# A gated mix of local and full attention on one core: the front's projections sum both row halves in one PSUM bank, in four banks that then go to the scores

## Chip, core and metric

One core of a Trainium2 chip. The metric is the device time in microseconds (us), as the median of several runs; smaller is better. Engines: TensorE (PE; PEld is its weight load), VectorE (DVE), ScalarE (ACT), GpSimd (POOL) and SyncE (SP, which issues DMAs). Matmuls write into PSUM, which has eight banks of 512 fp32 values in each of 128 partitions; GpSimd doesn't read PSUM in this kernel.

## What is computed

For one sequence of 2048 tokens of width 512, two attention branches and a gate:

```python
g = sigmoid((x * gate_w).sum(-1))
# branch A: 32 heads of 16; each token attends to 8 tokens, 2 apart, at and before it
qkv = x @ A_wqkv;  a = softmax(scale * q . k[pos - 2*w], w = 0..7) . v;  a = a @ A_wo
# branch B: 32 query heads of 16, one key and value head, all 2048 keys, no mask
q = x @ B_wq;  k = x @ B_wk;  v = x @ B_wv
b = softmax(q . k * 16 ** -0.5) . v;  b = b @ B_wo
out = g * a + (1 - g) * b
```

The softmax subtracts the row maximum, so all 32 x 2048 x 2048 scores of branch B are formed twice: once for their row maxima, once for the exponentials.

## The kernel before

**The work.** A projection in fp32 accuracy is three matmuls of split parts (high x high, high x low, low x high; `three`, line 168) for each of four 128-row blocks of the contraction: twelve products. Queries of branch B are split again and stored to DRAM (`qd`), and come back "stacked" as units: a unit is four heads by 512 queries, 32 units in all, of which eight are held at a time (`qst`). For a unit, `max_mm` forms scores for maxima with 512 keys in the free dimension, DVE reduces them, and the maxima are transposed and written into two spare contraction rows of the unit (`shift_a` to `shift_d`), so that the score matmul of `exp_pair` already subtracts them. 2048 such maxima tiles (128 rows by 512 keys) are needed, 64 for each unit, before that unit's turn.

**The front** (about 29 to 279 us). A list `lumps` holds 14 projections of queries (lumps `("q", m)`) and 64 of branch A (`("a", gg, j)`; 384 columns, and for gg 0 eighteen more, B's values and the gate). Each of a lump's twelve products is cut into its lower and upper 64 contraction rows, which the two row halves of PE work on at the same time. `stream` (line 660) is a planner: it keeps a model clock for PE, ACT and DVE (`clk`) with the durations of line 45 (`T_R`, `T_EXP`, ...), and issues for each slot one product to each half. Lower halves of lump x go to the first bank of a two-bank tile, upper halves to its second (line 1004; tiles `pe0` and `pe1` in turn, `pm` for the last lump). Into this it puts work on maxima where the model clock says that a bank is free:
- a *pair* (`fill_pair`): two matmuls into `pm`, one 1024-wide DVE reduction;
- a *single* (`fill_one`): one matmul in place of one half's product, into `ps` or `po`, one 512-wide reduction;
- from lump ("a", 0, 4) on, a *difference* (`fill_diff`, `fill_sum`): with keys prepared as half sums and half differences of two key blocks (`half_keys`), max(a, b) is half sum + |half difference|; two matmuls into `pm`, two ACT `Abs` into `dd`, then two matmuls into `ps` and `po` in place of one half's product each, and two DVE instructions that add and reduce. A difference stands for four maxima tiles.

At a lump's end ACT and POOL evict it. A query (`queries_post`, line 196): one ACT copy of both banks, a POOL addition of the halves, an ACT copy to the high part, a POOL subtraction for the low part, two DMAs. Branch A (`a_post`, line 226): an ACT copy of each bank, POOL additions, and for every second token block a DMA to DRAM (`ad`). Work for POOL and DMAs is queued in `tasks` with a due time. POOL otherwise computes branch A's local attention from `ad` (`work`, `run_pool`), from when the first quarter of branch A is stored until long after the front.

**The loop** (279 to 1510 us), 512 steps s: for each of 16 key blocks of each unit, two score pairs with their exponentials (`exp_pair`, tiles `pe0` and `pe1`, 1024-wide ACT), and the weighted sums of the step before (`weighted`, 128-row fp32 matmuls into `po`). In a step the planner places the members in the order of line 1068: scores 0, a pair ("m2"), scores 1, a single ("m1"), then the weighted sums. `fill_ready` (line 803) lets a pair or single in when its bank is free by the model, or will be within `M2S` or `M1S`; `singles` (line 799) allows singles only while more maxima are left than two for each remaining step. Three blocks of four rows of output projections (`out_phase`, also through `stream`) stand between steps, a fourth is spread over the last steps.

The first values of a unit's maxima tile (`unit_tile`, line 301) are set by an ACT instruction for units 0 to 8.

Of the kernel before, what the change touches and what calls it, by code (L numbers as in the profile page):

```python
# [6 lines left out]
F32 = mybir.dt.float32  # L7
# [34 lines left out]
LEAD, M2S, M1S = 1.5, 0.5, 0.3  # L42


T_R, T_LAT, T_EXP, T_RED2, T_RED1, T_W, T_TTR = 0.23, 0.20, 0.92, 1.14, 0.61, 1.21, 0.66
# [3 lines left out]
def gated_mix_kernel(ctx, tc, xt, wa, wk, wq, wo_a, wo_b, out):  # L49
# [19 lines left out]
    eb = [pp.tile([P, 2, 512], F32, name=f"pe{k}") for k in range(2)]  # L69
    m2 = pp.tile([P, 2, 512], F32, name="pm")  # L70
    m1 = pp.tile([P, 512], F32, name="ps")
    po = pp.tile([P, 512], F32, name="po")

# [97 lines left out]
    def keys(t):  # L171
        pk = eb[t % 2][:, 0, :]
# [23 lines left out]
    def queries_post(m, bank):  # L196

        nonlocal pool
        settle("rest", 0)
        two = p0.tile([P, 2, 512], F32, name="two", tag="wqr", bufs=1)  # L200
        nc.scalar.activation(two, bank, AF.Copy)
        at = after("act", clk["pe"] + T_LAT, 0.92)
        own = p0.tile([P, 512], F32, name="qraw", bufs=1)
        nc.gpsimd.tensor_add(own, two[:, 0], two[:, 1])
        pool = max(pool, 1e3 * at) + 1400
        hi, lo = parts_of()

        def rest():
            nonlocal pool
            nc.scalar.activation(hi, own, AF.Copy)  # L210
            nc.gpsimd.tensor_sub(lo, own, hi.bitcast(F32))
            pool = max(pool, 1e3 * after("act", 0, 0.6)) + 1400
            queries_out(m, hi, lo)
            if m > 4 and m % 2 and len(stacked) < NB:
                stack(len(stacked))

        tasks.append((pool / 1e3, rest, (), "rest"))
# [8 lines left out]
    def a_post(gg, j, x):  # L226

        nonlocal pool
        (bank, key), n = front[x], GN + (0 if gg else VN)
        settle("add", 1)  # L230
# [4 lines left out]
        if gg == 0 and j < 3:  # L235
            two = wp.tile([P, GN + VN], F32, name="two", tag="aext", bufs=2)
        else:
            two = (p2 if j % 3 else pm)[0].tile([P, GN + VN], F32, name="two", tag=("two", "raw", "own")[j % 3], bufs=1)
        own = st[:, :, j % 2, :]
        nc.scalar.activation(own, bank[:, 0, :GN].rearrange("p (g n) -> p g n", g=GC), AF.Copy)  # L240
        nc.scalar.activation(two[:, :n], bank[:, 1, :n], AF.Copy)  # L241
        if gg == 0:
            nc.scalar.activation(vst[:, j, 0:DH], bank[:, 0, GN:GN + DH], AF.Copy)
            nc.scalar.activation(gate[:, 1, j:j + 1], bank[:, 0, GN + DH:GN + DH + 1], AF.Copy)
        at = after("act", clk["pe"] + T_LAT, 0.8 if gg else 1.2)
        free[key] = at + 0.1

        def rest():
            nonlocal pool
            nc.gpsimd.tensor_add(own, own, two[:, :GN].rearrange("p (g n) -> p g n", g=GC))  # L250
            if gg == 0:
                nc.gpsimd.tensor_add(vst[:, j, 0:DH], vst[:, j, 0:DH], two[:, GN:GN + DH])
                nc.gpsimd.tensor_add(gate[:, 1, j:j + 1], gate[:, 1, j:j + 1], two[:, GN + DH:GN + DH + 1])
            pool = max(pool, 1e3 * at) + (1000 if gg else 1450)
            if j % 2 == 1:
                dst = ad[gg * GC:(gg + 1) * GC, HALO:, :].rearrange("g (p j) n -> p g (j n)", j=NJ)
                tasks.append((pool / 1e3 + 0.5, lambda: nc.sync.dma_start(dst[:, :, (j - 1) * AN:(j + 1) * AN], st.rearrange("p g j n -> p g (j n)")), (), "store"))
            if j == NJ - 1:
                tasks.append((pool / 1e3 + 1.0, whole, (gg,)))

        tasks.append((at, rest, (), "add"))
# [35 lines left out]

    def fillable():
        return bool(half) or bool(slots) and slots[0][0] < len(stacked) and stacked[slots[0][0]] <= clk["pe"]

    def unit_tile(v):
        if v not in mx:
            mx[v] = wp.tile([P, 2, 2, 4, 4], F32, name="mx", bufs=3)
            if v <= NB:
                nc.scalar.activation(mx[v].rearrange("p b i t k -> p (b i t k)"), ident[:, 0:64], AF.Identity, scale=0.0, bias=mk[:, 6:7])
            left[v] = NF // NU
# [9 lines left out]
    def filled(v, n):  # L316
        left[v] -= n
        if not left[v]:
# [4 lines left out]
            nc.vector.transpose(mt, ms.rearrange("p b x y -> p (b x y)"))  # L323
            tasks.append((after("dve", 0, 0.66) + (2.0 if kcd and not pe else 0.1), shift_a, (v, mt)))

    def fill_pair(dst, key):
# [4 lines left out]
        nc.vector.tensor_reduce(m[:, :, pr, t, kc], dst, AX.X, ALU.max)  # L331
        free[key] = after("dve", after("pe", 0, T_R) + T_LAT, T_RED2) + 0.08
        filled(v, 2)

    def fill_one(dst=m1, key="m1"):
# [6 lines left out]
        nc.vector.tensor_reduce(m[:, odd, pr, t, kc:kc + 1], dst, AX.X, ALU.max)  # L342
        free[key] = after("dve", after("pe", 0, T_R) + T_LAT, T_RED1) + 0.08
        filled(v, 1)
# [18 lines left out]
    def half_keys(g):  # L363

        keys = ("m2", "m2") if g == 0 else ("m1", "po")
# [26 lines left out]
    def fill_diff():  # L392
# [5 lines left out]
        for odd in range(2):  # L398
            nc.scalar.activation(dd[0][:, odd], m2[:, odd, :], AF.Abs)  # L399
            ready_d[odd] = after("act", at, 0.52) + 0.1  # L400
        free["m2"] = ready_d[1]
        pend.extend([(v, pr, t, kc, 0), (v, pr, t, kc, 1)])

    def fill_sum():
# [4 lines left out]
        nc.vector.tensor_tensor_reduce(dd[0][:, odd], dst, dd[0][:, odd], 1.0, -FMAX, ALU.add, ALU.max, m[:, odd, pr, t, kc:kc + 1])  # L409
# [754 lines left out]
```

## Time and profile before

| | |
|---|---|
| median of 3 runs | 1527.74 us (1527.43 to 1530.11) |
| span of the profiled execution, first to last instruction | 1523.8 us |
| PE, ACT, DVE, POOL busy over the span | 98%, 82%, 81%, 68% |
| front (first planned slot to the first steps' scores) | 29 to 279 us |
| granted TensorE clock, mean | 0.997 |

The profile is one execution; its span lies 3.9 us under the median, and only the span is recorded of it. A row of the timeline gives start, length, engine, line, operation, output and inputs, how many such instructions were merged (x2), and in brackets how long the engine had been idle before it and what ended that. A row of the groups gives count, then busy time in us and mean ns of one, then the idle time before them with its releasers. A row of waits gives total us, how often, the longest. PE's ends are modelled, so spacing of starts says more than length.

### The profile page before, as it was taken

What the parts mean: (1) busy time and instruction counts of PE and PEld (TensorE: products, weight loads), DVE (VectorE), ACT (ScalarE), POOL (GpSimd) and SP (SyncE); (2) the same over time, 40 slices, a digit from 0 to 9 for tenths busy, and PEclk for the clock granted to TensorE, in tenths of its full rate; (3) what the DMA queues carried; (4) which work ended last, traced back from release to release, by engine and by line L of the source; (5) the groups of instructions that cost most, each with busy time, mean ns of one, the idle gap of its engine ahead of it and who ended that gap; (6) DMA issues with size and microseconds to landing.
All of it is one profiled execution on the core that took longest, in us unless ns stands there. A gap on an engine that the chain in (4) does not pass through costs nothing.

```text
span 1523.8 us, 28901 instructions
## 1 busy us (share of the span) xinstructions
PE 1489.5 (98%) x10920; PEld 706.1 (46%) x10920; DVE 1235.3 (81%) x1755; ACT 1243.8 (82%) x1590; POOL 1030.6 (68%) x1769
## 2 busy tenths in 40 slices
PE   7999999999999999999999999999999999999988
PEld 4989888533333333333333453333345335433333
DVE  5976666788888888889888998898899889888701
ACT  4558987889999899999999759999975995799774
POOL 7866988787888888888888888889887004100020
PEclk9999999999999999999999999999999999999999
DMA  6744223121121121120220112202201000000000
GB/s 216 202 119 131 90 75 126 33 75 47 50 76 47 41 75 44 43 76 22 66 77 14 65 33 68 68 12 69 69 19 33 1 1 16 15 2 2 1 1 28
DMA packets 43908, 85.63 MB, mean 56 GB/s; under 512 B 9520, under 2 KB 25960, under 8 KB 39672
## 3 DMA queue, kind: packets, MB, share of 16 engines
q1 hardware_dynamic: 36200, 44.00, 9.8%
q0 software_dynamic: 6560, 37.95, 7.5%
q8 instruction: 86, 1.41, 0.4%
q10 hardware_dynamic: 1008, 1.84, 0.3%
q14 instruction: 54, 0.44, 0.1%
HBM read 57.97 MB, written 25.25 MB: 55 GB/s over the span
## 4 chain that ended last, share of the span: by engine, by line
PE 89%; ACT 4%; DVE 4%; POOL 1%; issue 1%; DMA 1%; DVEq 0%; ACTq 0%; POOLq 0%
PE po L458 32%; PE pe L448 22%; PE pm L311 9%; PE ps L311 8%; PE pe L1004 8%; PE pe L709 4%; DVE mx L331 2%; ACT dd L399 2%; ACT pexp L450 1%; PE pm L766 1%; PE pm L390 1%; PE pe L174 1%; DVE mx L342 1%; PE po L390 0%; PE ps L390 0%
## 5 line engine op out<-in xcount | busy, mean ns | idle before, releaser
L450 ACT ACTIVATE pexp<-pe 128x1024 f32<-128x1024 f32 x1024 | 992.9, 1022 | 116.3 <-PE pe L448 116.0
L331 DVE TENSOR_REDUCE mx<-pm 128x2 f32<-128x1024 f32 x554 | 676.6, 1221 | 125.7 <-PE pm L311 120.4
L458 PE MATMUL po<-pexp,vst 128*32 128x512 f32 x4096 | 547.1, 606 | 0.6 <-DVE tt L472 0.5
L448 PE MATMUL pe<-qst,kst 64*128 64x512 f32 x2048 | 460.9, 448 | 6.8 <-ACT pexp L450 2.6
L448 PEld LDWEIGHTS pe<-qst,kst 64*128 64x128 f32 x2048 | 190.6, 184 | 506.7 <-ACT pexp L450 488.4
L342 DVE TENSOR_REDUCE mx<-ps 128x1 f32<-128x512 f32 x565 | 384.4, 680 | 5.7 <-PE ps L311 5.0
L311 PE MATMUL pm<-kst,qst 62*128 62x512 f32 x1122 | 235.7, 407 | 3.1 <-DVE mx L331 2.4
L311 PE MATMUL ps<-kst,qst 62*128 62x512 f32 x565 | 228.6, 405 | 0.7 <-DVE mx L342 0.7
L518 POOL TENSOR_TENSOR pr<-aext 128x256 f32<-128x256 f32 x256 | 182.0, 736 | 0.2
L578 POOL TENSOR_TENSOR oa<-oa,av 128x256 f32<-128x256 f32 x224 | 163.9, 732 | 15.4
L458 PEld LDWEIGHTS po<-pexp,vst 128*32 128x32 f32 x4096 | 80.7, 108 | 182.5 <-issue 170.7
L575 POOL TENSOR_TENSOR av<-aext,lg 128x256 f32<-128x256 f32 x224 | 139.3, 622 | 12.8
L484 POOL TENSOR_TENSOR rl<-rl,gate_t 128x16 f32<-128x16 f32 x31 | 6.8, 220 | 182.6 <-DVE rl L478 182.4
L311 PEld LDWEIGHTS pm<-kst,qst 62*128 62x128 f32 x1122 | 108.9, 186 | 24.7 <-DVE mx L331 21.3
L311 PEld LDWEIGHTS ps<-kst,qst 62*128 62x128 f32 x565 | 105.3, 186 | 22.4 <-DVE mx L342 18.4
L399 ACT ACTIVATE dd<-pm 128x512 f32<-128x512 f32 x166 | 92.2, 610 | 21.8 <-DVE mx L409 10.8
L1004 PE MATMUL pe<-wah,xh 64*128 64x384 f32 (+1 forms) x504 | 108.5, 338 | 0.0
L1004 PE MATMUL pe<-wal,xh 64*128 64x384 f32 (+1 forms) x504 | 108.5, 337 | 0.0
L1004 PE MATMUL pe<-wah,xl 64*128 64x384 f32 (+1 forms) x504 | 108.4, 337 | 0.0
L409 DVE CUSTOM_DVE_ANT_0 dd<-ps,dd 128x512 f32<-128x512 f32 x83 | 57.4, 692 | 58.8 <-PE ps L390 29.4
L524 POOL TENSOR_TENSOR tr<-pr 128x512 f32<-128x512 f32 x64 | 81.7, 1276 | 4.2
L250 POOL TENSOR_TENSOR stage<-stage,two 128x384 f32<-128x384 f32 x64 | 65.0, 1015 | 26.3 <-ACT two L241 13.4
(185 smaller groups left out, 1596.7 us busy)
## 6 DMA issues: line engine op xcount, KB each, us to landing
aext<-ad POOLq DMA_DIRECT2D x32, 1056.0 KB, 5.4
ad<-stage SPq DMA_DIRECT2D x32, 384.0 KB
qst<-qd SPq DMA_DIRECT2D x64, 128.0 KB
xraw<-xt SPq DMA_DIRECT2D x16, 256.0 KB
qd<-qhi SPq DMA_DIRECT2D x16, 256.0 KB
qd<-qlo SPq DMA_DIRECT2D x16, 256.0 KB
qst<-qd SPq DMA_DIRECT2D x64, 64.0 KB
qst<-ml SPq DMA_DIRECT2D x228, 2.0 KB
```

The lines of the kernel that those rows point to most:

```text
L311: nc.tensor.matmul(dst, qst[v % NB][b:b + 62, pr, t * P:(t + 1) * P], kst[b:b + 62, kc * 512:(kc + 1) * 512], start=True, stop=True)
L331: nc.vector.tensor_reduce(m[:, :, pr, t, kc], dst, AX.X, ALU.max)
L342: nc.vector.tensor_reduce(m[:, odd, pr, t, kc:kc + 1], dst, AX.X, ALU.max)
L399: nc.scalar.activation(dd[0][:, odd], m2[:, odd, :], AF.Abs)
L448: nc.tensor.matmul(bank[:, odd, :], kst[b:b + 64, kt * P:(kt + 1) * P], qst[u % NB][b:b + 64, pr, :], start=True, stop=True)
L450: nc.scalar.activation(e, bank, AF.Exp, scale=SCALE)
L458: nc.tensor.matmul(po[32 * i:32 * i + 32, :], vst[:, kt, :], pexp[s, i // 2][:, i % 2, :], start=(kt == 0), stop=(kt == NJ - 1))
L518: nc.gpsimd.tensor_mul(pr[:, k], q, e[:, o:o + NH, AC:2 * AC])
L524: nc.gpsimd.tensor_add(nx, cur[:, :, 0:n], cur[:, :, n:2 * n])
L575: nc.gpsimd.tensor_mul(av, e[:, o:o + NH, 2 * AC:].rearrange("p j (h d) -> p j h d", d=DH), lg[:, w].unsqueeze(3).to_broadcast([P, NH, AG, ...
L578: nc.gpsimd.tensor_add(ao, ao, av)
L1004: nc.tensor.matmul(front[2 if x == last else x % 2][0][:, b, :n], l[h], r[h], start=(i == 0), stop=(i == 3 * C - 1))
```

## The change

- **Front outputs in one bank.** Both row halves of a lump accumulate into one bank (`start` only for the lower half's first product, `stop` for the upper half's last). Four one-bank tiles `pf0` to `pf3` take the lumps in turn; the last two lumps use `po` and `ps`. The two halves never work on one lump at a time: the upper half's first matmul gets a wait for an instruction on ACT or DVE (`mark`, `behind`) that itself follows PE work issued after the lower half's last product. So the lower half runs at least a lump ahead. A new planner, `front_stream`, advances the two halves separately (`below`: the bank must be free; `after_upper`: a mark must exist).
- **Evictions.** A query is copied twice by ACT straight from the bank (itself and its high part); POOL only subtracts. Branch A takes one ACT copy (and two small ones for gg 0); its POOL additions are gone, and the DMA is due 0.3 us after ACT.
- **Banks given back.** After the last lump but two, the four tiles are released and `pe0`, `pe1` for the scores are allocated over them; the first scores are issued at the last lump's tenth product of the upper half.
- **First values.** Units 0 and 1 as before; 2 to 8 by a GpSimd memset, asked for when the unit two before is complete.
- **Order in a step.** Scores 0, pair, single, scores 1.
- **Planner.** A difference also waits for ACT's model clock (`ACTS`); `T_R` is 0.235 instead of 0.23, `T_TTR` (the add-and-reduce) 0.74 instead of 0.66; the halved-keys step waits until its banks are free (`wanted`).

```diff
-T_R, T_LAT, T_EXP, T_RED2, T_RED1, T_W, T_TTR = 0.23, 0.20, 0.92, 1.14, 0.61, 1.21, 0.66
+ACTS, LEAD, M2S, M1S = 0.5, 1.5, 0.5, 0.3
+T_R, T_LAT, T_EXP, T_RED2, T_RED1, T_W, T_TTR = 0.235, 0.20, 0.92, 1.14, 0.61, 1.21, 0.74
...
-    eb = [pp.tile([P, 2, 512], F32, name=f"pe{k}") for k in range(2)]
+    pf = tc.alloc_tile_pool(name="outputs", bufs=1, space=PSUM, side="right")
+    fb = [pf.tile([P, 512], F32, name=f"pf{k}") for k in range(4)]
...
     def queries_post(m, bank, key):
-        nc.scalar.activation(two, bank, AF.Copy)
-        nc.gpsimd.tensor_add(own, two[:, 0], two[:, 1])
+        nc.scalar.activation(own, bank, AF.Copy)
+        nc.scalar.activation(hi, bank, AF.Copy)
...
     def a_post(gg, j, bank, key):
-        nc.scalar.activation(own, bank[:, 0, :GN].rearrange("p (g n) -> p g n", g=GC), AF.Copy)
-        nc.scalar.activation(two[:, :n], bank[:, 1, :n], AF.Copy)
+        nc.scalar.activation(st[:, :, j % 2, :], bank[:, :GN].rearrange("p (g n) -> p g n", g=GC), AF.Copy)
...
-            nc.gpsimd.tensor_add(own, own, two[:, :GN].rearrange("p (g n) -> p g n", g=GC))
...
-            if v <= NB:
+            if v < 2:
                 nc.scalar.activation(mx[v].rearrange("p b i t k -> p (b i t k)"), ident[:, 0:64], AF.Identity, scale=0.0, bias=mk[:, 6:7])
+            elif v <= NB:
+                nc.gpsimd.memset(mx[v], -FMAX)
...
     def mm(b, at):
-        nc.tensor.matmul(front[2 if x == last else x % 2][0][:, b, :n], l[h], r[h], start=(i == 0), stop=(i == 3 * C - 1))
+        inst = nc.tensor.matmul(home(x)[0][:, :n], l[h], r[h], start=(i == 0 and b == 0), stop=(i == 3 * C - 1 and b == 1))
+        if b == 0 and x == last - 2 and i == 3 * C - 4:
+            ended.add(1)
+        if b == 1 and i == 0:
+            tc.add_manual_dep(inst.ins, behind(x), mybir.DependencyInfo(mybir.DependencyClass.Sync, mybir.DependencyReason.DATA))
...
+    def front_stream(seq):
...
+            for b in (0, 1) if odd != 1 else (1, 0):
+                if b == odd:
+                    now = clk["pe"]
+                    single()
+                    clk["pe"] = now
+                elif at[b] < len(seq) and may[b](*seq[at[b]]):
+                    dur = max(dur, mm(b, seq[at[b]]))
+                    at[b] += 1
...
+                if not half and not pend and not wanted and max(free["m2"], clk["dve"] - 1.2, clk["act"] - ACTS) <= clk["pe"] + 0.1:
+                    fill_diff()
...
+    def behind(x):
+        marks[:] = [m for m in marks if m[0] > x]
+        return next((m[2] for m in marks if m[1] + 0.1 <= clk["pe"]), None)
+
+    def after_upper(x, i):
+        return i > 0 or behind(x) is not None
+
+    def below(x, i):
+        return i > 0 or free.get(home(x)[1], 0.0) <= clk["pe"] + 0.1 and (lumps[x] != ("a", 0, 3) or bool(pm)) and not (pend and x >= last - 1)
...
-        order = (0, "m2", 1, "m1") if s > 1 else (1, "m2", 0, "m1") if s else ()
+        order = (0, "m2", "m1", 1) if s > 1 else (1, "m2", "m1", 0) if s else ()
```

More of the change, by code (lines that the diff above doesn't have):

```diff
@@ L684, in stream @@
             after("pe", 0, dur or T_R)
-            if ended:
-                pass
-            elif paired():
-                if not half and not pend and max(free["m2"], clk["dve"] - 1.2) <= clk["pe"] + 0.1:
-                    fill_diff()
-            elif slots and fillable() and free["m2"] <= clk["pe"] + 0.1:
+            if slots and fillable() and free["m2"] <= clk["pe"] + 0.1:
                 clk["pe"] = max(clk["pe"], free["m2"])
@@ L989, in mm @@
         if x not in items:
[L990 to L1000 removed]
+            begin(x)
         n = 512 if lump[0] == "q" else GN + (0 if lump[1] else VN)
```

190 lines of the change are left out of this document (113 added, 77 removed).

## The prediction

> **What bounds the kernel now.** I read the page's head and its chain of work that ended last, then the busy time by stage, and then the timeline of single steps, because the averages mix two stages with different limits.
>
> ```profile
> span 1523.8 us, 28901 instructions
> PE 1489.5 (98%) x10920; PEld 706.1 (46%) x10920; DVE 1235.3 (81%) x1755; ACT 1243.8 (82%) x1590; POOL 1030.6 (68%) x1769
> PE 89%; ACT 4%; DVE 4%; POOL 1%; issue 1%; DMA 1%; DVEq 0%; ACTq 0%; POOLq 0%
> ```
>
> TensorE (PE) carries 89% of the chain, so a change pays only where it takes time out of PE's own sequence. Stages, as columns: stretch, its length, busy PE, weight loads, DVE, ACT, POOL, granted clock, DMA share, GB/s.
>
> ```profile
> 29.00:81.00 52.00, 50.36 (x424) 44.80 (x425) 51.35 (x66) 26.74 (x37) 45.06 (x39) 1.00 0.65 181
> 105.00:279.00 174.00, 170.30 (x1696) 153.27 (x1693) 112.79 (x349) 146.13 (x340) 138.59 (x226) 1.00 0.34 104
> 279.00:1434.00 1155.00, 1147.98 (x8127) 444.61 (x8125) 1025.72 (x1260) 991.88 (x1091) 798.64 (x1437) 1.00 0.13 41
> ...
> 1200.00:1400.00 200.00, 199.36 (x1440) 81.97 (x1439) 178.62 (x213) 161.78 (x177) 33.25 (x52) 1.00 0.02 7
> ```
>
> The front ends at 279. While queries are projected (29 to 81) DVE is full, 51 of 52 us; while branch A is projected (105 to 279) ACT is fullest after PE, 146 of 174, or 84%. The last row is a part of the third: POOL has run out of work by then. In the loop the rows of one step matter:
>
> ```profile
> 423.68 1.23 DVE L331 TENSOR_REDUCE mx<-pm 128x2 f32<-128x1024 f32 x1 [0.27 <-PE pm L311]
> ...
> 424.04 1.07 PE L458 MATMUL po<-pexp,vst 128*32 128x512 f32 x8
> 424.82 0.68 DVE L342 TENSOR_REDUCE mx<-ps 128x1 f32<-128x512 f32 x1
> ...
> 425.04 0.50 PE L448 MATMUL pe<-qst,kst 64*128 64x512 f32 x2
> ...
> 425.37 0.41 PE L311 MATMUL pm<-kst,qst 62*128 62x512 f32 x2
> 425.49 0.19 PEld L448 LDWEIGHTS pe<-qst,kst 64*128 64x128 f32 x2 [0.16 <-ACT pexp L450]
> 425.60 0.41 PE L448 MATMUL pe<-qst,kst 64*128 64x512 f32 x2
> ...
> 425.81 1.23 DVE L331 TENSOR_REDUCE mx<-pm 128x2 f32<-128x1024 f32 x1 [0.31 <-PE pm L311]
> 425.85 0.40 PE L311 MATMUL ps<-kst,qst 62*128 62x512 f32 x1
> ...
> 426.17 1.07 PE L458 MATMUL po<-pexp,vst 128*32 128x512 f32 x8
> ```
>
> Weighted sums to weighted sums is 2.13 us (424.04 to 426.17): first scores 1.00 later, pair 0.33, second scores 0.23, single 0.25, weighted sums 0.32. PE has no hole in it. A step in which the planner placed no single:
>
> ```profile
> 937.78 1.06 PE L458 MATMUL po<-pexp,vst 128*32 128x512 f32 x8
> ...
> 939.35 0.39 PE L448 MATMUL pe<-qst,kst 64*128 64x512 f32 x2
> ...
> 939.67 1.07 PE L458 MATMUL po<-pexp,vst 128*32 128x512 f32 x8
> ```
>
> It is 1.89 us long, so **a single costs 0.24 us in the loop**, for half a pair's maxima. What the front fills in advance is what the loop need not fill with singles.
>
> **The change part by part.** The groups of the front (29 to 279), columns as on the page:
>
> ```profile
> L399 ACT ACTIVATE dd<-pm 128x512 f32<-128x512 f32 x166 | 92.2, 610 | 21.8 <-DVE mx L409 10.8 <-PE pm L390 10.6
> L250 POOL TENSOR_TENSOR stage<-stage,two 128x384 f32<-128x384 f32 x63 | 64.0, 1015 | 26.0 <-ACT two L241 13.1 <-ACT vst L243 12.1 <-DVE mx L409 0.6
> L409 DVE CUSTOM_DVE_ANT_0 dd<-ps,dd 128x512 f32<-128x512 f32 x83 | 57.4, 692 | 58.8 <-PE ps L390 29.4 <-ACT dd L399 21.1 <-ACT mx L305 5.4
> L331 DVE TENSOR_REDUCE mx<-pm 128x2 f32<-128x1024 f32 x28 | 34.2, 1223 | 5.2 <-PE pm L311 5.2
> L241 ACT ACTIVATE two<-pe 128x384 f32<-128x384 f32 (+1 forms) x63 | 31.5, 499 | 0.0
> L204 POOL TENSOR_TENSOR qraw<-two 128x512 f32<-128x512 f32 x14 | 18.1, 1291 | 2.4 <-DVE mx L342 0.9 <-ACT two L201 0.5 <-PE pm L311 0.3
> L342 DVE TENSOR_REDUCE mx<-po 128x1 f32<-128x512 f32 x26 | 17.9, 690 | 0.0
> L342 DVE TENSOR_REDUCE mx<-ps 128x1 f32<-128x512 f32 x26 | 17.9, 690 | 0.0
> L201 ACT ACTIVATE two<-pe 128x1024 f32<-128x1024 f32 x14 | 14.4, 1027 | 5.7 <-PE pe L1004 5.1
> ```
>
> Maxima filled by the front: 28 pairs of two, 52 singles, 83 differences of four, 440 of 2048.
>
> *Evictions.* Gone are 64 copies of the second half (64 x 0.50 = 32 us of ACT) and 64 additions on POOL (65 us), and of each query the two-bank copy (1.03 us) and its addition (1.29). A query keeps its second copy and takes 512 columns instead of 1024 in the first; the nearest row for that is L399, 0.61, so ACT has 14 x 0.42 = 6 us less. POOL loses 83 us; worth nothing by itself, since it already runs dry before the end, and the blocks of output rows that wait for branch A take PE as long earlier as later. The stores wait for ACT and no more for POOL; the same DMAs leave the same queue a microsecond sooner.
>
> *First values* of seven maxima tiles move from ACT to POOL, asked for a unit ahead. DVE's 5.4 us of waits for them (L305 in the row of L409) go; they lie in idle time of DVE, so I count nothing. If POOL lagged by a whole unit, one DVE instruction would wait, seven times at most: under 5 us.
>
> *What ACT's time turns into.* In the front a difference is a chain: matmul pair, two ACT Abs, two sums on DVE, and only then the next difference. Evictions sit in ACT's queue between them.
>
> ```profile
> DVE dd L409 <- PE ps L390: 29.4, 43, 2.5
> DVE dd L409 <- ACT dd L399: 21.1, 27, 2.1
> ACT qhi L210 <- POOL qraw L204: 14.1, 10, 2.5
> PEld pm L390 <- ACT dd L399: 13.6, 39, 1.6
> ```
>
> 83 differences in 174 us are one in 2.1 us. Bounds for how many more fit: none, if DVE were the limit, and 17, since only eight units of queries are stacked in the front (512 maxima, 72 above 440). DVE is 65% busy from 105 to 279 (113 of 174), and a sum row is 0.69, so DVE allows them; the 32 us off ACT are worth 26 differences of two Abs at 0.61. Towards the end the planner stops differences one lump earlier than now and lets pairs go. I take the middle: 10 more differences and 5 more pairs: **50 maxima**, bounds 20 and 70.
>
> Their price in the front, by spacing of starts:
>
> ```profile
> 164.47 0.34 PE L1004 MATMUL pe<-wah,xh 64*128 64x384 f32 x2
> ...
> 164.64 0.34 PE L1004 MATMUL pe<-wal,xh 64*128 64x384 f32 x2
> ```
>
> Two 384-wide halves take 0.17 us together; two 512-wide ones take 0.23 (425.37 to 425.60 above). A difference is one slot of 0.23 for its two matmuls and half a slot for each sum, 0.47; ten are 4.7, five pairs 1.2: **+5.9**. In the loop 50 singles fewer are 50 x 0.24: **-12.0**. That singles go and not pairs follows from line 801: a single is placed only while more is left than two maxima per remaining step.
>
> *Stalls in the front.* PE's weight loads for a difference wait 13.6 us in all for ACT (39 times), because ACT is behind an eviction. Halved evictions and the planner's new test on ACT (ACTS) take most of that: **-9**, bounds 0 and -14. What is late next is DVE, whose sums the planner now charges 0.74 (0.66 before; the row says 0.69 and its readout 0.08 more).
>
> *The skew.* The lower halves start a lump ahead, and each upper half's first matmul waits for an ACT or DVE instruction that came behind the lower half's last. Everything on PE is queued behind that wait, scores and maxima alike. At the start the array is half used for a lump of twelve 0.23 slots and a bit, at the end for some twenty of 0.17: half of 3.5 us twice, less what singles use of it: **+3**. Bounds: +1, and +8 with all four banks' lead. A mark that comes later on the chip than in the plan would stall PE at each of 78 lumps; with the lead once built up the mark lies a lump back, so I count none.
>
> A lump's two halves start together now (x2 in each row above), each in its bank. The Trainium skill, TensorEngine Tiling (Array Packing), section Restrictions and Gotchas, says that different row tiles cannot access the same PSUM bank at the same time and that software has to keep them apart. The change keeps to that by the skew; no row of before shows two halves in one bank. Were the halves of a lump simply to follow each other with nothing beside them, it would be the third rival.
>
> *Hand-over.* The scores' banks are the front's four, free only when the last lumps have left them; the first scores start at the upper half's tenth product instead of the third, seven slots of 0.17: **+1**, bounds 0 and +3.
>
> *Single between pair and scores.* PE's sequence has the same members, so nothing is removed from the 2.13. What moves is the slack. Now the single starts at 425.85, 0.35 after DVE left its bank (424.82 + 0.68 = 425.50). Moved ahead of the second scores it is due at 425.60, 0.10 after. What that is worth shows where a single did wait:
>
> ```profile
> 420.75 0.68 DVE L342 TENSOR_REDUCE mx<-ps 128x1 f32<-128x512 f32 x1
> ...
> 421.47 0.18 PEld L311 LDWEIGHTS ps<-kst,qst 62*128 62x128 f32 x1 [0.29 <-DVE mx L342]
> 421.48 0.50 PE L311 MATMUL ps<-kst,qst 62*128 62x512 f32 x1
> ...
> 421.90 1.07 PE L458 MATMUL po<-pexp,vst 128*32 128x512 f32 x8
> ```
>
> DVE ends at 421.43, the load starts 0.05 later, and the next matmuls come 0.42 after the single instead of 0.32: 0.15 from DVE's end to streaming. So the moved single would be 0.05 late. Going round: pair to single is 0.44 (425.37 to 425.81) + 1.14 + 0.68 + 0.15 = 2.41; single to the pair after next's turn is 0.23 + 0.32 + 1.00 + 0.33 = 1.88; two steps are 4.29, a step 2.15 against 2.13. Upper end: 0.02 over some 450 singles, 9 us, and 0.1 for each of two steps in every one of 32 units, in which DVE has transposes besides, 7 more: +16. Lower end: second scores that wait for ACT (the load at 425.49 did, within its cover) then have a single ahead of them that uses the wait: -3. A margin of 0.05 is as small as the error of these differences, and where DVE is much behind, the planner's test (M1S) skips the single rather than wait; I take **+4**.
>
> *The stop before the last steps.* At 1434 the plan ran out of steps and stopped to fill:
>
> ```profile
> 1437.85 0.80 PE L448 MATMUL pe<-qst,kst 64*128 64x512 f32 x2 [1.77 <-DVE mx L331]
> ```
>
> Fewer maxima left to do shorten this stop: **-2**, bounds 0 and -5.
>
> **Sum:** 5.9 - 12.0 - 9 + 3 + 1 + 4 - 2 = -9.1 us on a span of 1523.8. The median of the runs, 1527.7, is 3.9 above that span, which I leave as it is: **1519 us** (-0.6%).
>
> **The rivals.**
> 1. *The single's bank becomes the wait (slower).* The mechanism is the 2.41 above, at every step with a single after a step with one. All else as forecast is -13.1, so it decides from 13.1 / 450 = 0.03 us per step on. At its upper end of +16 it gives +3, 1531; with 30 maxima instead of 50 (0.24 less 0.47 / 4, 0.12 each, +2.4) and stalls of -5 instead of -9 besides, +9, 1537. For it: DVE's row at 424.82 ends 0.10 before the single would be due. Against: DVE still has 0.3 us of idle in a step ([0.31 <-PE pm L311]), and skipped singles release it.
> 2. *ACT's time is not turned into maxima (no change).* If differences stay bound by their own chain, Abs to sum to Abs (DVE's 29.4 and 21.1 us of waits are that chain), the planner adds few: 15 maxima net -1.8, stalls -4, skew, hand-over and order +8, stop 0: 1530, and with order at 0, 1526. That the change does not do what it says would end here too.
> 3. *The halves take turns.* 14 lumps of twelve slots of 0.23 and 64 of 0.17 are 170 us when both halves stream together; with each lump's halves one after the other and nothing beside them, up to 170 us more, near 1700. The four banks speak against it: the lower half always has a free one to go on in.
>
> **How the numbers follow.** A measurement of this kernel tells about 0.2% (3 us) from no change. Faster than that, the forecast's case: 0.57. Within it, the second rival and the mild end of the first: 0.16. Slower, the first rival and with 0.02 the third: 0.27. The forecast's own range is 1504 (70 maxima, -2.4; stalls at -14, -5; order at -3, -7) to 1524. With the second rival and the first up to its end the range is **1504 to 1537**.
>
> **What would show it.** Right: about 93 differences in the front (186 Abs instead of 166), some 50 fewer single reductions in the loop, the front ending within 4 us of 279, loads for differences waiting for ACT under 6 us. Wrong: the front ending past 284, with PE waiting at the first product of upper halves for DVE or ACT; the loop's step at 2.15 or more, with loads for singles waiting for DVE in most steps; steps after a DVE transpose longer than now.

## The result: slower by 0.7%, and the profile after

The changed kernel takes **1538.61 us** (median; 1536.40 to 1540.16), the kernel before 1527.95 beside it: ratio **1.0068, 95% interval 1.0054 to 1.0082**. I had forecast 1519 and a range of 1504 to 1537. The profiled execution took 1539.97, its span is 1538.1 (before 1523.8), so 14.3 us have to be found in the trace. The head of the page after, and the chain that ended last:

```profile
span 1538.1 us, 28700 instructions
...
PE 1500.0 (98%) x10920; PEld 713.8 (46%) x10920; DVE 1231.8 (80%) x1736; ACT 1218.1 (79%) x1531; POOL 948.2 (62%) x1670
...
PE 91%; DVE 4%; ACT 3%; DMA 1%; issue 1%; POOL 0%; SPq 0%; DVEq 0%; ACTq 0%; POOLq 0%
```

PE has the same number of matmuls, 10920, and is busy 10.5 us longer. ACT lost 25.7 us of work and POOL 82.4, as the change meant; none of that is in the time. The stretches after, with columns as in the prediction (length, busy PE, weight loads, DVE, ACT, POOL, granted clock, DMA share, GB/s):

```profile
29.00:92.50 63.50, 58.93 (x449) 52.99 (x450) 60.73 (x73) 18.11 (x35) 29.00 (x27) 0.89 0.56 155
92.50:288.00 195.50, 192.63 (x1912) 179.35 (x1911) 142.76 (x407) 141.79 (x323) 123.78 (x235) 1.00 0.37 115
288.00:340.00 52.00, 46.14 (x292) 15.27 (x292) 27.13 (x36) 41.36 (x46) 44.30 (x90) 0.93 0.16 44
340.00:1447.00 1107.00, 1102.50 (x7798) 422.08 (x7796) 971.05 (x1168) 949.19 (x1039) 718.04 (x1280) 1.00 0.12 39
31.30:44.90 13.60, 9.59 (x36) 7.15 (x36) 11.79 (x9) 0.00 (x0) 4.66 (x4) 0.51 0.18 55
331.70:338.40 6.70, 5.45 (x20) 2.14 (x20) 2.23 (x3) 1.80 (x2) 5.99 (x10) 0.51 0.20 40
```

Two things are new: query projection ends at 92.5 instead of 81, and the granted clock, 1.00 in every such stretch of before, is about one half for 13.6 us there and for 6.7 us at 332. The last query product and the first weighted sums fix the ends of the front's two halves; before:

```profile
81.01 0.39 PE L1004 MATMUL pe<-xh,wql 64*128 64x512 f32 x1
...
279.45 1.06 PE L458 MATMUL po<-pexp,vst 128*32 128x512 f32 x8
```

After:

```profile
92.33 0.39 PE L999 MATMUL pf<-xh,wql 64*128 64x512 f32 x1
...
288.18 1.06 PE L455 MATMUL po<-pexp,vst 128*32 128x512 f32 x8
```

So the query half costs 11.3 us more, and branch A's half, with most of the 38 extra maxima, 2.6 us less (195.85 against 198.44). In the same way I read the start of single steps off the timelines, for these two kernels and for the ones that the experiments below compare (us; a step is numbered by the weighted sums that end it, one less than the kernel's `s`; "others" is each kernel's span less the rows above):

| stretch | before | after | old order (e1) | four edits (e8) | e8 with the change's order (e11) |
|---|---|---|---|---|---|
| to the first weighted sums | 279.5 | 288.2 | 287.6 | 283.0 | 280.7 |
| steps 0 to 20 | 45.4 | 51.5 | 49.6 | 43.2 | 43.8 |
| steps 21 to 488, three output phases included | 1116.0 | 1115.9 | 1107.6 | 1107.5 | 1123.6 |
| steps 489 to 511 | 70.5 | 70.2 | 70.5 | 70.5 | 70.5 |
| others (last outputs) | 12.4 | 12.3 | 11.0 | 10.9 | 11.0 |

The whole loss lies ahead of step 21: +8.7 and +6.1. The 468 steps that were to give back 12 us gave nothing. That nothing is itself a sum: 39 steps more went without a single (42 against 3), the steps that had one took longer (2.16 us in the median instead of 2.13), and the stop before the last steps grew (10.1 us for that step instead of 6.6). The rows of the weight loads for singles show the first two; columns: count, busy us and mean ns, idle us before them and who ended most of it; stretch 345 to 1430. Before:

```profile
L311 PEld LDWEIGHTS ps<-kst,qst 62*128 62x128 f32 x506 | 94.3, 186 | 19.9 <-DVE mx L342 16.3
```

After:

```profile
L300 PEld LDWEIGHTS ps<-kst,qst 62*128 62x128 f32 x467 | 85.6, 183 | 83.0 <-DVE mx L334 79.2
```

39 singles fewer (506 to 467), and loads for singles wait nearly five times as long for DVE (79.2 us against 16.3), the wait that the first rival named. Of the 42 steps without one, 29 are the second of a unit, behind DVE's transpose of the weighted sums. Three losses, then, each with a theory to test: the **start** of the front, the **ninth stacked unit** in steps 0 to 20, and the **order** in the loop.

### The profile page after: what moved, and what is told of

Same layout as the page of the kernel before. It is cut to its first block, busy times and chain, and to the rows that moved or that the text cites. A ratio compares the mean times of both kernels' runs of the same rounds, so it can differ in the third digit from the quotient of the medians.

```text
span 1538.1 us, 28700 instructions
## 1 busy us (share of the span) xinstructions
PE 1500.0 (98%) x10920; PEld 713.8 (46%) x10920; DVE 1231.8 (80%) x1736; ACT 1218.1 (79%) x1531; POOL 948.2 (62%) x1670
## 4 chain that ended last, share of the span: by engine, by line
PE 91%; DVE 4%; ACT 3%; DMA 1%; issue 1%; POOL 0%; SPq 0%; DVEq 0%; ACTq 0%; POOLq 0%
PE po L455 32%; PE pe L444 24%; PE pf L999 10%; PE pm L300 9%; PE ps L300 5%; PE pe L693 4%; DVE mx L322 2%; ACT pexp L446 2%; PE pm L384 1%; PE pm L750 1%; PE pf L177 1%; PE po L384 1%; PE ps L384 1%; DVE mx L334 1%; DMA qd<-qlo 0%
## 5 line engine op out<-in xcount | busy, mean ns | idle before, releaser
L322 DVE TENSOR_REDUCE mx<-pm 128x2 f32<-128x1024 f32 x570 | 696.1, 1221 | 155.7 <-PE pm L300 144.0
L444 PE MATMUL pe<-qst,kst 64*128 64x512 f32 x2048 | 570.4, 456 | 7.3 <-ACT pexp L446 2.9
L444 PEld LDWEIGHTS pe<-qst,kst 64*128 64x128 f32 x2048 | 234.0, 184 | 445.5 <-ACT pexp L446 429.3
L334 DVE TENSOR_REDUCE mx<-ps 128x1 f32<-128x512 f32 x516 | 350.5, 679 | 0.0
L300 PE MATMUL pm<-kst,qst 62*128 62x512 f32 x1142 | 247.8, 412 | 12.3 <-DVE mx L322 6.8
L575 POOL TENSOR_TENSOR oa<-oa,av 128x256 f32<-128x256 f32 x224 | 164.1, 732 | 15.9
L999 PE MATMUL pf<-wah,xh 64*128 64x384 f32 (+1 forms) x496 | 142.8, 338 | 0.0
L999 PE MATMUL pf<-wah,xl 64*128 64x384 f32 (+1 forms) x496 | 142.2, 337 | 0.0
L999 PE MATMUL pf<-wal,xh 64*128 64x384 f32 (+1 forms) x496 | 142.2, 337 | 0.0
L300 PEld LDWEIGHTS pm<-kst,qst 62*128 62x128 f32 x1142 | 113.4, 187 | 37.4 <-DVE mx L322 25.7
L999 PEld LDWEIGHTS pf<-wah,xl 64*128 64x128 f32 x496 | 88.6, 186 | 1.6 <-issue 0.4
L999 PEld LDWEIGHTS pf<-wah,xh 64*128 64x128 f32 x496 | 88.2, 186 | 1.4 <-issue 0.4
```

The lines of the kernel that those rows point to most:

```text
L300: nc.tensor.matmul(dst, qst[v % NB][b:b + 62, pr, t * P:(t + 1) * P], kst[b:b + 62, kc * 512:(kc + 1) * 512], start=True, stop=True)
L322: got = nc.vector.tensor_reduce(m[:, :, pr, t, kc], dst, AX.X, ALU.max)
L334: got = nc.vector.tensor_reduce(m[:, odd, pr, t, kc:kc + 1], dst, AX.X, ALU.max)
L444: nc.tensor.matmul(bank[:, odd, :], kst[b:b + 64, kt * P:(kt + 1) * P], qst[u % NB][b:b + 64, pr, :], start=True, stop=True)
L575: nc.gpsimd.tensor_add(ao, ao, av)
L999: inst = nc.tensor.matmul(home(x)[0][:, :n], l[h], r[h], start=(i == 0 and b == 0), stop=(i == 3 * C - 1 and b == 1))
```

## The experiments

### The order alone, undone and done (e1, e2, e3)

Undone in the kernel after:

```diff
-        order = (0, "m2", "m1", 1) if s > 1 else (1, "m2", "m1", 0) if s else ()
+        order = (0, "m2", 1, "m1") if s > 1 else (1, "m2", 0, "m1") if s else ()
```

> The change with the old order in a step (scores, pair, scores, single). Theory A (the moved single waits for DVE to leave its bank, some 0.02 to 0.04 us in each step that has one): the loop from step 21 to 488 gets about 9 us shorter, 1529 us in all, steps with a single back at 2.13, loads for singles wait for DVE under 25 us in all instead of 83. Rival B (the order is neutral, and the loop gains nothing because fewer singles are no gain): within 2 us of the change, 1537 to 1540.

1530.21 us, ratio 1.0013 (1.0003 to 1.0022): 8.4 us under the kernel after. Loads for singles wait as before:

```profile
L300 PEld LDWEIGHTS ps<-kst,qst 62*128 62x128 f32 x495 | 92.2, 186 | 18.8 <-DVE mx L334 14.5
```

28 singles come back, and steps 21 to 488 take 1107.6 instead of 1115.9. So the order was a cost, not the mild one that I had put down.

Done in the kernel before, and nothing else of the change:

```diff
-        order = (0, "m2", 1, "m1") if s > 1 else (1, "m2", 0, "m1") if s else ()
+        order = (0, "m2", "m1", 1) if s > 1 else (1, "m2", "m1", 0) if s else ()
```

> The kernel before with only the new order in a step. Theory A: 8 to 12 us slower than before, 1536 to 1540, steps with a single at 2.15 to 2.17, loads for singles wait for DVE some 80 us in all. Rival B: within 2 us of before.

1550.67, ratio 1.0146 (1.0132 to 1.0159): 22 us, twice the forecast, and nearly three times what the same edit costs inside the change. Its line of waits (total us, times, longest), same stretch, shows the same wait as in the kernel after:

```profile
PEld ps L311 <- DVE mx L342: 76.5, 357, 0.5
```

What differs is the end: 40 steps went without a single (3 before), and the maxima that they left were made up in stops at `s` = 457, 473 and 489, which took 10.1, 15.9 and 13.5 us, at a halved clock in part. In the change, 38 maxima more had been filled in the front, and by these counts they stood in for singles that the plan dropped: **the front's gain was there and paid for the order.**

The third kernel puts the single ahead of the pair, again in the kernel before:

```diff
-        order = (0, "m2", 1, "m1") if s > 1 else (1, "m2", 0, "m1") if s else ()
+        order = (0, "m1", "m2", 1) if s > 1 else (1, "m1", "m2", 0) if s else ()
```

> The kernel before with the order scores, single, pair, scores. DVE then reduces the single first and leaves its bank more than 1 us before it is needed; the second scores come as late as in the change's order. Theory A (it is the single's bank): 1526 to 1531, steps at 2.13. Rival C (it is the second scores that come 0.24 us later and hold up ACT): as slow as the change's order alone, 1536 to 1540.

1551.08, ratio 1.0152 (1.0138 to 1.0166), where 1526 to 1531 was expected: a miss. Rival C had it as slow as the order of e2, and the time fits that. Its mechanism doesn't: loads for scores wait less for ACT than before (353.9 us in all against 442.2, in e2 374.4). Instead the pair's bank is late now:

```profile
PEld pm L311 <- DVE mx L331: 95.7, 396, 0.9
...
PEld ps L311 <- DVE mx L342: 8.9, 26, 0.8
```

DVE works in the order in which PE fills: here single first, then pair. Whichever of the two stands last before the second scores has its bank back only after 0.68 + 1.23 us of DVE, and waits for it in most steps. It isn't the single that was wrongly placed; between the first and the second scores there is room for one of the two.

### Is it the wait, or what the plan does about it? (e9, e11)

The plan drops a single when its bank would come free more than 0.3 us late (M1S). So the order could cost through the wait in each step, or through the dropped singles and their stop. In the kernel after:

```diff
-ACTS, LEAD, M2S, M1S = 0.5, 1.5, 0.5, 0.3
+ACTS, LEAD, M2S, M1S = 0.5, 1.5, 0.5, 0.8
```

> The kernel after, with one number of the plan changed: a single is issued if its bank comes free within 0.8 us by the plan instead of within 0.3 us. It keeps 27 of the singles that the new order makes the plan drop, with 5 pairs fewer. Theory D (the order costs its 9 us through the dropped singles: the maxima they leave, 42 steps without a single against 23 with the old order, are made up in one stop of 10.1 us before the last steps): the stop of 10.13 us goes or falls under 4 us, the steps get longer by 27 times 0.17 = 4.6 us at most, and the time is 3 to 6 us under after's (1532 to 1536). Theory C (the order costs through the wait for the single's bank in every step): each single that is kept waits the 0.3 to 0.5 us that the plan had seen, the steps get longer by 27 times 0.5 = 13 us, and the time is not under after's (1538 to 1543).

1544.58, ratio 1.0115 (1.0099 to 1.0130): slower by 6 us than the kernel after, the way theory C has it and above its range of 1538 to 1543. The stop of 10.1 us is gone, as theory D had it, but the singles that are kept pay more than that:

```profile
L300 PEld LDWEIGHTS ps<-kst,qst 62*128 62x128 f32 x500 | 91.8, 184 | 99.2 <-DVE mx L334 94.9
```

The cleanest comparison is with the other losses mended (e8, below): the same kernel in both orders, with as many singles in each (for that the new order has M1S at 0.8).

```diff
-ACTS, LEAD, M2S, M1S = 0.5, 1.5, 0.5, 0.3
+ACTS, LEAD, M2S, M1S = 0.5, 1.5, 0.5, 0.8
...
-        order = (0, "m2", 1, "m1") if s > 1 else (1, "m2", 0, "m1") if s else ()
+        order = (0, "m2", "m1", 1) if s > 1 else (1, "m2", "m1", 0) if s else ()
```

> The kernel with four edits, but with the change's own order (pair, single, second scores) and the single issued if its bank comes free within 0.8 us by the plan, so that it issues as many singles as the old order does (502 against 503 in the loop's rows that differ, pairs 495 against 494). Theory D (only the dropped singles cost): 1517 to 1520, as the kernel with four edits. Theory C (the bank's wait in each step costs by itself): the median step with a single is 2.155 to 2.16 us against 2.130, so 450 times 0.025 to 0.03 = 11 to 13 us more, 1529 to 1531.

1533.47, ratio 1.0035 (1.0023 to 1.0048), against 1517.95 for the old order: **15.5 us for the order with the singles kept** (14.4 by the two ratios, since the two were timed beside different runs of the kernel before). In the two traces steps 21 to 488 differ by 16.1. Old order first, new order second:

```profile
L300 PEld LDWEIGHTS ps<-kst,qst 62*128 62x128 f32 x502 | 93.5, 186 | 19.2 <-DVE mx L334 15.3
```

```profile
L300 PEld LDWEIGHTS ps<-kst,qst 62*128 62x128 f32 x501 | 91.9, 184 | 99.4 <-DVE mx L334 95.7
```

One step of each. Old order:

```profile
602.72 1.06 PE L455 MATMUL po<-pexp,vst 128*32 128x512 f32 x8
603.51 0.68 DVE L334 TENSOR_REDUCE mx<-ps 128x1 f32<-128x512 f32 x1
...
604.06 0.40 PE L300 MATMUL pm<-kst,qst 62*128 62x512 f32 x2
604.29 0.40 PE L444 MATMUL pe<-qst,kst 64*128 64x512 f32 x2
604.30 0.19 PEld L300 LDWEIGHTS ps<-kst,qst 62*128 62x128 f32 x1
...
604.52 0.40 PE L300 MATMUL ps<-kst,qst 62*128 62x512 f32 x1
604.85 1.06 PE L455 MATMUL po<-pexp,vst 128*32 128x512 f32 x8
```

New order:

```profile
603.44 1.07 PE L455 MATMUL po<-pexp,vst 128*32 128x512 f32 x8
604.22 0.68 DVE L334 TENSOR_REDUCE mx<-ps 128x1 f32<-128x512 f32 x1
...
604.78 0.40 PE L300 MATMUL pm<-kst,qst 62*128 62x512 f32 x2
604.96 0.18 PEld L300 LDWEIGHTS ps<-kst,qst 62*128 62x128 f32 x1 [0.22 <-DVE mx L334]
605.01 0.45 PE L300 MATMUL ps<-kst,qst 62*128 62x512 f32 x1
605.01 0.67 PE L444 MATMUL pe<-qst,kst 64*128 64x512 f32 x2
...
605.61 1.07 PE L455 MATMUL po<-pexp,vst 128*32 128x512 f32 x8
```

In the old order DVE has left the single's bank at 604.19 and the load comes 0.11 later without a wait; the step is 2.13. In the new one DVE leaves it at 604.90, the load comes 0.06 later and the matmul 0.11, everything behind it on PE moves with it, and the step is 2.17. Over the 453 and 454 steps with a single the mean is 2.152 against 2.188 and the median 2.130 against 2.160.

### The start of the front (e4, e5)

The rows of the start after: POOL subtracts for the last split of the inputs in one piece, DVE splits the query weights beside it (two inputs from SBUF), PE waits for the maxima queued behind that on DVE.

```profile
25.48 0.68 DVE L79 TENSOR_TENSOR wql<-wqr,wqh 128x512 fp32r<-128x512 f32 x1
25.95 10.01 POOL L79 TENSOR_TENSOR xl<-xraw,xh 128x512 fp32r<-128x512 f32 x8 [4.62 <-ACT xh L78]
...
31.19 5.32 DVE L79 TENSOR_TENSOR wql<-wqr,wqh 128x512 fp32r<-128x512 f32 x1
...
37.70 0.80 PE L300 MATMUL pm<-kst,qst 62*128 62x512 f32 x2 [4.01 <-DVE mx L322]
```

The same subtraction takes DVE 0.68 just ahead of POOL's run and 5.32 in the middle of POOL's eight. It ends at 36.51, POOL at 35.96. Before, POOL came in two pieces of four, and the split took 1.48:

```profile
31.02 5.47 POOL L76 TENSOR_TENSOR xl<-xraw,xh 128x512 fp32r<-128x512 f32 x4 [0.25 <-ACT xh L75]
...
32.64 1.48 DVE L76 TENSOR_TENSOR wql<-wqr,wqh 128x512 fp32r<-128x512 f32 x1
...
35.31 0.50 PE L311 MATMUL pm<-kst,qst 62*128 62x512 f32 x2 [1.10 <-DVE mx L331]
```

The Trainium skill, SBUF — State Buffer, section SBUF: two separate sides, says that a VectorE instruction with two SBUF inputs and a GpSimd instruction that reads SBUF share one pair of ports, which the first holds for its whole instruction. The trace agrees, and goes further: 5.32 us is longer than any one of POOL's eight (10.01 / 8 = 1.25), so DVE was passed over for several in a row. The traces of e1, e6 and e9, in which the front is the same, show it too (5.30 to 5.33).

The other half of the theory is the skew itself: in the first lump only the lower halves of the array have products. First test, give the upper half twelve products into a bank that is free (their result is overwritten, no output changes):

```diff
+        if b == 0 and x == 0:
+            nc.tensor.matmul(fb[2], l[64:128], r[64:128], start=True, stop=True)
```

> The change; while the lower halves work on the first lump, the upper half of the array forms the same 12 products into a bank that nobody reads. Theory A (the granted clock falls to one half at 31.3 because the array is half used in the stretch before): the clock stays at 1.00 to 45 us, the front ends 5 to 7 us sooner, 1531 to 1534. Rival D (the clock falls because PE waits 4 us for DVE there): the clock is still halved near 31 to 45, and the time stays within 2 us of the change.

1535.65, ratio 1.0045 (1.0033 to 1.0058): 3 us less, where 1531 to 1534 was expected. The last query product is at 86.4 instead of 92.3, and the clock is halved for 3.4 us there. DVE's split was short as well, which the edit hadn't meant:

```profile
25.49 10.50 POOL L79 TENSOR_TENSOR xl<-xraw,xh 128x512 fp32r<-128x512 f32 x8 [4.63 <-ACT xh L78]
...
30.73 1.66 DVE L79 TENSOR_TENSOR wql<-wqr,wqh 128x512 fp32r<-128x512 f32 x1
...
33.58 0.50 PE L300 MATMUL pm<-kst,qst 62*128 62x512 f32 x2 [1.06 <-DVE mx L322]
```

POOL's eight still follow each other without a gap, and DVE gets in after one of them (in e7, with the same front, it is 1.64). So a run of eight doesn't always hold DVE for 5.3 us, and what decides it is open. Nor does this run part the two causes. The second test leaves the upper half idle and moves POOL's last four subtractions from ahead of the front's stream to behind its second query block:

```diff
-    split_x(3, nc.gpsimd)
...
+            if x == 1:
+                split_x(3, nc.gpsimd)
```

> The kernel after, but GpSimd's subtractions for the last split of the front (8 of them, 10.01 us in one piece in the trace after) are issued two query blocks later, behind the first stretch of the front in which VectorE's split of the query weights took 5.32 us beside them. Theory A (the slow start comes from VectorE being held by GpSimd's reads: TensorE waited 4.0 us for a maximum behind that split): the split falls to 0.7 to 1.7 us, TensorE's wait to 1 us or less, the granted clock is halved for less than 13.65 us, query products end at 86 to 89 instead of 92.3, and the time is 3 to 6 us under after's (1532.5 to 1535.5). Theory B (the half array alone lowers the clock, whatever VectorE does): the split gets short but the clock is still halved for 10 us or more; gain 0 to 2 us.

1536.17, ratio 1.0055 (1.0041 to 1.0069): 2.4 us less. The split is 0.68 and the wait is gone, yet matmuls still take 0.79 a little later, at a clock that is halved for 6.8 us instead of 13.7:

```profile
31.41 0.68 DVE L79 TENSOR_TENSOR wql<-wqr,wqh 128x512 fp32r<-128x512 f32 x1
...
34.47 0.79 PE L300 MATMUL po<-kst,qst 62*128 62x512 f32 x1
```

By the ratios alone neither gain is clear of the kernel after (1.0054 to 1.0082), but the traces repeat. The last query product is at 90.5 to 92.3 in the four with the change's front (after, e1, e6, e9), at 86.3 and 86.4 with the upper half filled (e7, e4), at 88.4 with POOL's work moved (e5), and at 85.2 to 85.7 with both (e8, e10, e11). So the half-used array costs by itself: with POOL's work moved, filling the upper half still gains 2.7 us or more. Nor does PE's long wait start the halved clock, as rival D of e4 had it: in the kernel after the clock falls at 31.5 and the wait begins at 33.7. Moving POOL's work gains 2.1 us or more beside an idle upper half, and 0.6 beside a filled one (86.3 to 85.7). In e8, and in e10 and e11 too, no stretch of the front up to 80 us is below full clock; e8:

```profile
0.00:40.00 40.00, 33.27 (x140) 19.60 (x141) 26.12 (x43) 15.55 (x28) 22.46 (x27) 1.00 0.65 206
40.00:80.00 40.00, 38.96 (x334) 36.22 (x332) 38.77 (x51) 14.90 (x29) 24.14 (x22) 1.00 0.67 189
```

The Trainium skill, TensorE: Matmul & The Clock Gate, section Part 1: The HAM clock gate, has the clock fall to half after a window of some 3.4 us in which the array is idle. The trace agrees on the halves and on steps of 3.4 us (3.4, 6.8, 10.2 and 13.7 here); that a half-used array can be enough, with no wait of PE over 0.3 us, is what e5 adds.

### The ninth unit (e6)

Eight units of queries are stacked in the front. The kernel after has filled 478 of their 512 maxima there and the rest by `s` = 13; from 13 to 19 no step gets a pair. The ninth unit's buffer is free only at `s` = 17, at 322 us, and SP issues its four DMAs behind the eight of a shift:

```profile
320.60 5.22 SPq L432 DMA_DIRECT2D qst<-ml  x8
...
325.92 0.61 SPq L266 DMA_DIRECT2D qst<-qd  x1
...
327.88 0.58 SPq L267 DMA_DIRECT2D qst<-qd  x1
...
332.86 0.29 PEld L300 LDWEIGHTS pm<-kst,qst 62*128 62x128 f32 x1 [4.68 <-DMA qst<-qd]
332.89 1.62 PE L300 MATMUL pm<-kst,qst 62*128 62x512 f32 x2 [4.38 <-DMA qst<-qd]
```

The plan counts on 5 us from there to use; the DMAs start 4 us later and take 7 from the first one on, and all of PE's work stands behind that pair. The clock is halved for 6.8 us (the last row of the stretches above). One number is changed, for this unit alone:

```diff
-        stacked.append(clk["pe"] + 5.0)
+        stacked.append(clk["pe"] + (11.0 if len(stacked) == NB else 5.0))
```

> The kernel after, with one number of the plan changed: the ninth stacked unit counts as ready 11 us after its stacking is issued instead of 5 us, so that no pair or single is put in front of TensorE before its DMAs have landed (in the trace after they landed 7 us after being issued, behind the shift DMAs, and the pair's weight load waited 4.68 us). Theory A (the loss of 6.2 us in steps 0 to 20 is this stop and the halved clock that follows it): no such wait, no halved clock near 331 to 338, and the time 4 to 7 us under after's (1531.5 to 1534.5). Theory B (the maxima that the stop delays are owed anyway and come back as a longer stop at the end): the wait goes, the loop's end stop before the last steps grows by as much, and the time is within 2 us of after's.

1539.60, ratio 1.0085 (1.0072 to 1.0098): nothing gained. Theory A was right on the place, since steps 0 to 20 take 43.9 us instead of 51.5, and theory B on the time: the loop takes 8.0 more. In the kernel after the stop before the last steps is this one (10.1 us for that step):

```profile
1447.40 0.50 PE L300 MATMUL pe<-kst,qst 62*128 62x512 f32 x2 [0.92 <-DVE mx L322]
1448.53 0.50 PE L300 MATMUL pm<-kst,qst 62*128 62x512 f32 x2 [0.63 <-DVE mx L322]
...
1453.05 0.79 PE L444 MATMUL pe<-qst,kst 64*128 64x512 f32 x2 [1.52 <-DVE mx L322]
```

With the ninth unit later it is 15.5 us long, with another of 6.2 at `s` = 473, and the clock averages 0.70 around it:

```profile
1437.00:1460.00 23.00, 16.80 (x81) 5.80 (x77) 15.08 (x16) 8.70 (x13) 1.00 (x1) 0.70 0.00 1
```

In a stop DVE alone sets the pace, 1.13 us for a pair, and a maximum costs 0.57 us where a single in a step costs 0.24. As long as the order leaves the loop short of singles, what is lost elsewhere is made up in such a stop: steps 0 to 20 placed six maxima fewer, and the two stops together are 9.5 us longer, in part for the halved clock.

### The edits together (e7, e8), and one part undone (e10)

The kernel after with the edits of e1, e4 and e6, as shown above: old order, upper half kept busy, ninth unit at 11 us.

> The kernel after with three edits at once: the old order in a step (pair, then second scores, then single), the upper half of the array kept busy in the first stretch of the front, and the ninth unit counted as ready 11 us after its stacking. If the three losses are separate (order 8.4 us, start 3.0 us, ninth unit 4 to 7 us), the sum is 1520 to 1523.5, under the kernel before by 4 to 8 us (ratio 0.995 to 0.997). If the time that the start and the ninth unit cost is taken up by another wait once the order is mended, it stays at 1526 to 1530.

**1517.95, ratio 0.9939 (0.9926 to 0.9952)**: 20.7 us under the kernel after, twice the 10.4 that the three edits gave one by one (8.4 + 3.0 - 1.0), and 10 under the kernel before. With the old order there is no stop at `s` = 489 any more, and so the ninth unit's 6.4 us in steps 0 to 20 (49.6 to 43.2) are kept. It beats both kernels.

With the edit of e5, POOL's split put later, as a fourth:

> As the kernel with three edits, with GpSimd's last subtractions put two query blocks later as well. If GpSimd's reads still cost the start something when the upper half is busy (VectorE's split 1.66 us there, TensorE's wait 1.06 us), 1 to 2 us under the kernel with three edits; if the upper half was all of it, the same within 1 us; slower by 1 to 3 us if the last query blocks then wait for the split that was put off.

1517.95, ratio 0.9941 (0.9928 to 0.9954): the same. The clock is full up to the end of the loop, but the 0.6 us of the query half that this gives (85.70 against 86.31) is below what can be told.

In that kernel ScalarE wrote the maxima's first values again:

```diff
-            if v < 2:
+            if v <= NB:
                 nc.scalar.activation(mx[v].rearrange("p b i t k -> p (b i t k)"), ident[:, 0:64], AF.Identity, scale=0.0, bias=mk[:, 6:7])
-            elif v <= NB:
-                nc.gpsimd.memset(mx[v], -FMAX)
```

> The kernel with four edits, with the first values of the maxima of units 2 to 8 set by ScalarE again, as before, instead of by GpSimd's memset. My prediction put this part of the change at nothing: within 2 us of the kernel with four edits (1516 to 1520). If ScalarE's seven writes hold the front's evictions back, 1520 or more.

1519.82, ratio 0.9946 (0.9934 to 0.9959): the intervals overlap almost wholly. This part of the change is worth nothing that can be told, as forecast.

## Why the prediction was wrong

By the terms of the sum, the front was to cost 0.9 us net and cost 8.7; all that follows it was to give 10.0 and cost 5.6. One by one:

- **Extra maxima in the front (50, bounds 20 to 70): right, and fewer than forecast.** 440 became 478, so 38: seven pairs and six differences more. The second rival, with 15 maxima and stalls of -4, is out.
- **Stalls (-9): right.** Loads for differences wait 3.4 us for ACT instead of 13.6, so -10.2; from 105 to 290:

```profile
PEld pm L384 <- ACT dd L393: 3.4, 10, 0.6
```

- **First values (nothing), and the halves taking turns (third rival): right, and no sign of it.**
- **Skew (+3, bounds 1 to 8): the failure of a step.** I counted the half-used array as lost slots and left out what else hangs on the start. The half-used array lowered the clock, and DVE's split, held for 5.3 us beside POOL's subtractions, kept PE waiting for 4.0. The query half grew by 11.3 us, with both mended by 4.7 (81.0 to 85.7). Part of those 4.7 is no loss: 23 products of branch A are done by then, none before. The whole front with both mended is 1.3 to 3.8 us longer (e8, e10, e11), against 0.9 in the sum.
- **The loop's -12.0: the second failure.** I bounded what the front may fill by the 512 maxima of eight stacked units, and stopped there. At 478 the loop reaches that bound at `s` = 13, before the ninth unit can come: about half of the 38 are saved in steps 1 to 20, where the plan has nothing to place, and then PE waits for the DMA, so that these steps take 6.1 us longer. The loop proper is asked for only 18 fewer.
- **Order (+4, bounds -3 to +16): the step that decided.** My own chain had 2.15 against 2.13 and an upper end of 16, and I took a quarter of that because the margin was small and the planner would skip singles. Measured with the singles kept it is 15.5 (e11 against e8), the upper end, and the step's median is 2.16. The error was to call the wait small in a step and not to price the maxima that skipped singles leave: skipping did release the wait, for the price of the stop, 8.4 us with the change's surplus of maxima (e1), 22 without (e2).
- **Stop before the last steps (-2): wrong in sign** in the change, 10.1 us instead of 6.6, because of the skipped singles; right in sign with the old order, where there is none.
- **The signs.** Those of the first rival came: steps of 2.16, and loads for singles waiting for DVE in 372 of 467 cases. One sign of being right came too, in part by luck: 49 single reductions fewer (565 to 516). Of these 23 come back with the old order (539 in e1), so the plan had dropped them for the wait.
- **The first rival** was the right mechanism, and with 1531 to 1537 too cheap by the start and the ninth unit. For all but the order I had -13.1; with the order undone and the two other faults mended the median is 10.0 below before (e7). So the gains together were sized about right: in e8 all that follows the front is 12.2 us shorter than before, where the loop and the stop were forecast at -14.0 without the order. What was missing are the two faults, and the order's price was taken at the wrong end.

Open: how far the clock depends on the share of the array in use, since no run varied that share in steps; why POOL's run of eight held DVE's subtraction for 5.3 us in four traces and for 1.65 in two; and how the 4.7 us by which the query half of e8 is still longer divide into skew, extra maxima and work moved ahead.

## What to carry to other kernels

When a chain worked out from rows says that a wait appears in every step by 0.02 us, don't discount it for being small: times 450 it is 9 us, as much as the whole gain forecast here. And ask of work done in advance not only how much fits, but whether the next consumer can start when it runs out. Losses in a planned kernel aren't additive: mend the one that leaves the plan short first, or what is mended elsewhere comes back at the price of the last stop.

## What the runs showed of the hardware

- A DVE subtraction with two SBUF inputs took 0.68 us alone. Beside a run of eight POOL subtractions back to back it took 5.30 to 5.33 us in four traces (after, e1, e6, e9) and 1.66 and 1.64 in two (e4, e7); beside a run of four, 1.48 (before).
- PE's granted clock fell to one half for 6.8 us with the lower half of the array working and no wait of PE over 0.3 us (e5; at full clock with the upper half filled, e8), and for 6.8 us around a wait of 4.4 us for a DMA; a matmul's row then reads 0.62 instead of 0.39.
